# Summing two spectral products on VectorE ahead of the second half's inverse step, with a new hand-fixed order

## The chip, the cores and the metric

The kernel runs on one core of one Trainium2 chip. The metric is the time of one launch on the device in microseconds (us), lower is better. A core has five engines with queues of their own, which run at the same time and wait for each other through semaphores: PE (matrix multiply, TensorE), DVE (VectorE), ACT (ScalarE), POOL (GpSimd) and SP, which here only issues transfers (DMA). Matmul results land in PSUM, eight banks of 128 x 512 fp32, and DVE or ACT must copy or consume them before a bank can be used again.

## What is computed

Two blocks follow each other on a sequence of S = 2048 rows and D = 512 columns, in bf16. The first is a gated long convolution by FFT, the second a normalised mixer with an MLP. Cut to what matters:

```python
x = A_q;  qn = layernorm(x)
k_shift = sum over 4 taps of shifted k * shift_k
kv = k_shift * v
y = irfft(rfft(pad(kv)) * rfft(pad(ssm_k)))[:S] + kv * ssm_D      # length 2S
h = x + qn * y
u = layernorm(h);  h1 = gelu(layernorm(u) @ w1)                   # four column groups, shifted by -1, +1, -2, +2 rows
x1 = u + concat(shifted groups) @ w2
out = h + x1 + gelu(layernorm(x1) @ w3) @ w4                      # F = 1792
```

## The kernel before, in words

The rows are split into two halves, s = 0 and s = 1, of eight blocks of 128 rows each. Four signals are transformed: the filter's two halves (F0, F1) and kv's two halves (A0, A1). Each goes through the same stages, all matmuls with small trigonometric tables as weights, and a task in the code is one such step for one slice:

- S1 (`forward1`, `step1`, L389): the first transform step, evicted from PSUM by a copy E1 (`copy`, L257); X (L405): eight transfers from SBUF to SBUF that regroup the rows; S2 (`forward2`, L413): the second step, evicted by E2 (for F1 the eviction adds F0 in the same instruction, L425).
- P (`conv`, L474): the spectral products on DVE, 128 x 2048 bf16 each. The result of the first half needs one product of signals (A0 F0), that of the second two (A0 F1 and A1 F0). For each of four slices kl and each of two arrangements x of real and imaginary parts a product is one instruction: 8 for the first half, 16 for the second.
- I2 (L484): the inverse's first step on PE, 16 matmuls of 32 x 64 weights for each product, all products of a slice accumulating in the same four PSUM banks. EV copies the four banks out (L257, two copies), XI (L495) regroups by two transfers, I1 (L502) is the last inverse step, two blocks a time.

K and KV (L442, L450) make kv: matmuls with diagonal matrices of the taps (`dg`, L307 on DVE or L299 on POOL) and a product with v. Q (`qstat`, L506) takes the statistics of a block of q, QV, QP, QN (`qvar`, `qpow`, `qnorm`) turn them into scale and shift, Y (L613) normalises it. H (L616) joins q and y into h, one instruction on DVE for each block; HS (L600 or L602) takes its statistics; uw, rr, hn turn them into scale and shift (DVE and POOL); hb (L653, L655) writes the normalised block. LT and TE transpose it, some pairs of blocks with PE (L670 and a copy), five pairs of the two normalisations with transfers (`turn`: two writes to DRAM, L663, and a transposing read, L665). W and U (L699, L703) are w1 and its gelu, X2 and S (L722, L725) are w2 and its sum, SS, ux, r1, xn, lb, LX, EX repeat statistics, normalisation and transposes, M and G (L777, L781) are w3 and gelu, O and Z (L790, L792) are w4 and the last sum, OUT writes a block. R (L729) adds the residual.

All of these are about 780 tasks of a planner class, `Plan`. Nothing decides an order on the chip: the string ORDER lists the tasks, each with its engine letter and the numbers of the buffers it takes (PSUM banks, product buffers and others). `Plan.emit` goes through that list, so each engine runs its tasks in the order of the list, and a task that isn't ready holds up everything behind it on its engine. The numbers such as `{V: 1.15}` are the planner's costs in us, used outside this file when the list was made. A `port` note tells the planner of operations that use VectorE's and GpSimd's access to SBUF.

Around the change the order is as follows. The first half's convolution ends in I1 for s = 0, then H, W and X2 of the first half run while the second half's spectra are formed. From I2 of the second half on PE works off slice by slice, with M, G and O tasks of the first half's MLP between as other work. After its last I2 come two O tasks, then I1 for s = 1, then M tasks, two LT tasks and two O tasks, then W and X2 of the second half. After W of the second half almost only MLP matmuls remain.

Of the kernel before, what the change touches and what calls it, by code (L numbers as in the profile page):

```python
# [9 lines left out]
P = 128  # L10
S = 2048
D = 512
# [3 lines left out]
NB = 8  # L16
XW = 258
KW = NB * 129 + 8
# [13 lines left out]
004S 029P0 000S 002S 003S 005S 008S 031V 037V 001S 030P 063P23 006S 055P45 009S 057P67 064V 007S 056A 038G 065P01 010S 058A 019S 059P45 033V 045G  # L32
061P23 060A 087P60 039G 036V 062A 095P71 046V 042V 066A 093P4 032G 043V 047A 074S 101P5 044A 034G 015S 094V 051P23 022S 088V 053P01 035G 023S 052A
040V 072S 089P4 024S 054A 049G 091P6 021S 090V 073S 041A 097P2 096V 050G 070S 092V 099P3 048A 069S 102V 068S 107P01 098V 109P67 017S 100V 108A 103P45
067S 110V 111P23 018S 104A 115P01 071S 113P67 112A 323V 105P45 324V 116A 211P20 106V 114A 117P01 212V 119S 118A 084P4567 326V 085A 081P2301 123S 329V
086V 120S 083A 215P4 020S 082A 330V 124S 078P0167 327V 125S 217P5 080A 216V 121S 079A 075P2367 012S 218V 011S 325V 076A 127P4501 016S 319V 328V 122S
077A 219P21 129V 126S 331G 128A 013S 220V 130P6701 139V01 132A 141V23 131A 133P4501 332G 134A 140P23670 147V45 142P 135A 333G 149V67 143A 337G0
148P45011 155V01 150P 343G1 144A 145S 221P2 340G2 157V23 152A 146S 334G3 014S 151A 136P6701 222V 137V 138A 156P23452 153S 158P 154S 163V45 225P0 159A
223P1 160A 165V67 161S 164P67230 162S 226V 166P 224V 175P45 167A 168V 213P0 176A 169S 183P67 214V 170S 185P23 184A 187P45 315S 186V 177P01 188A 189P67
178V 179P23 190A 181P45 180V 171P67 028S 182A 172P01 338V 192S 231P45 196S 335V 339A 349G0 173P23 316S 344V 336A 346G3 193S 341V 235P67 232A 355G1  # L40
195S 347V 174P10 236A 352G2 191S 350V 237P45 198S 358G 342A 356V 202P6723 197S 348A 353V 194S 345A 359G 204V 239P01 238A 371G 203V 241P23 240A 227P45
242A 229P01 372G 360V 228V 230A 199P6723 247S 361G0 373V 233P45 351A 364G1 200V 362P00 234A 374G2 365P1 384V 366A 377G3 208P6745 245S 363V 354A 375P11
243S 201V 385G 367P0 376A 244S 357A 378P1 386V 246S 369P2 379A 390V0 318S 209V 397G 387A1 382P3 248S 370A 250S 388P12 210V 368A 398G 391P6 249S 380P7
383A 389A 027S 392V 399G 251P2345 263V01 381A 393P0 253A 026S 400G3 265V23 395P1 025S 252A 317S 403V2 205P6745 396A 267V45 401P23 394A 404P3 502P1
402A 206V 405A 506P0 503V 408P2 507V 504A 406P3 269V67 508A 409A 264P67011 558V 407A 266P 207V 268P 559G 270P 560G 498P2 271A 272V 561G1 510P3 564G0
499V 274S 494P4 501V 273S 562P50 511V 565P6 514P7 563A 495V 566A 411V 254P0123 496A 567P50 515V 256A 275V01 569P4 568A 577P6 277V23 570A 257P2345 578A
412V 573P7 259A 255V 571P6 258A 279V45 579P4 572A 574A 281V67 575P5 580A 516A 276P01232 414V 500A 278P 513V 280P 576A 615G 512V 282P 581P6 505V 283A
# [46 lines left out]
def body(ctx, tc, fx, kt, q, v, sd, w1, w2, w3, w4, out):  # L94
# [200 lines left out]
    def dg(c):  # L295
        def f(e, sl):
            if e == GP:
                tap = r_k[:, c * KW + NB * 129:(c + 1) * KW].rearrange("p (j x) -> p j x", x=2)[:, :, 1:2]
                pool.affine_select(out=diag[:, c], in_=tap.to_broadcast([P, 4, P]), compare_op=OP.is_equal, fill=0.0, base=0,  # L299
                                   pattern=[[0, 4], [-1, P]], channel_multiplier=1)  # L300
                return
# [542 lines left out]
```

## Time and profile before

| what | value |
|---|---|
| median of 3 runs | 213.93 us (213.45 to 215.72) |
| the profiled execution's own time | 213.26 us |
| its span, first to last instruction | 211.6 us |
| what lies around the span | 1.66 us |
| PE busy | 195.7 us, 93% |
| DVE busy | 144.8 us, 68% |
| ACT busy | 125.5 us, 59% |
| POOL busy | 80.1 us, 38% |

The profile's page has six parts. Part 1 gives busy time, part 2 cuts the span into 40 slices of 5.29 us and gives the busy share of each engine in tenths, part 4 is the chain of work that ended last, part 5 groups instructions by line, engine and tile. Other views used below are the chain in order of time, the timeline of one engine (start, duration, operation, and in brackets how long the engine was idle before it and on whom it waited), and a table of stretches of the span. PE takes in work all through the span, so what counts is in which stretch another engine keeps it waiting.

### The profile page before, as it was taken

Reading aid. Unit: us, or ns where it says so; the run is one execution under the profiler, and the core shown is the slowest. Engines: PE = TensorE matmul, PEld = TensorE weight load, DVE = VectorE, ACT = ScalarE, POOL = GpSimd, SP = SyncE. Lnnn points to the kernel's source line nnn. Section 1 sums busy time; section 2 is a strip of 40 time slices with the busy share of each in tenths; the row PEclk is TensorE's granted clock in tenths of the full one; section 3 lists DMA queues with packets and bytes.
Section 4 is the critical chain, followed back from the end, with each engine's and each line's share of the span. In section 5 each row is a group of like instructions: output and inputs, shape, how many; then the busy total and the mean of one; then the engine's idle time right before and its main releaser. Section 6 shows DMA issues by size and latency. Waiting matters only on the chain.

```text
span 211.6 us, 5040 instructions
## 1 busy us (share of the span) xinstructions
PE 195.7 (93%) x1964; PEld 116.2 (55%) x1980; DVE 144.8 (68%) x302; ACT 125.5 (59%) x206; POOL 80.1 (38%) x177
## 2 busy tenths in 40 slices
PE   6899769898889999979999999989999999999992
PEld 5454323442248546636744884645848888645450
DVE  6998999999999999999868971559972000112031
ACT  3979989787999658943751883364623565301010
POOL 7850059804888140287044683212765000000000
PEclk9999999999999999999999999999999999999999
DMA  6999895976948995000693008533146440010011
GB/s 173 313 403 397 321 325 222 256 205 237 371 169 294 332 435 147 0 28 13 89 232 92 27 22 181 98 69 82 42 107 154 102 74 0 3 50 34 16 50 50
DMA packets 30809, 32.86 MB, mean 155 GB/s; under 512 B 20545, under 2 KB 22594, under 8 KB 30530
## 3 DMA queue, kind: packets, MB, share of 16 engines
q1 hardware_dynamic: 30786, 32.55, 50.8%
q8 instruction: 15, 0.25, 0.5%
q14 instruction: 8, 0.07, 0.1%
HBM read 13.14 MB, written 4.46 MB: 83 GB/s over the span
## 4 chain that ended last, share of the span: by engine, by line
PE 59%; DVE 13%; ACT 12%; DMA 6%; issue 3%; POOL 3%; SPq 3%; DVEq 0%; ACTq 0%; POOLq 0%
PE ps L777 21%; PE ps L790 18%; ACT r_a L257 5%; PE ps L722 5%; PE ps L699 5%; PE ps L484 3%; DVE r_v L616 3%; DMA r_dg<-dhb 2%; DMA r_a<-r_a 2%; PE ps L502 2%; PE ps L413 2%; DMA r_k<-in_kt_dram 2%; DVE r_f L425 2%; DVE r_dg L307 1%; DVE r_p L474 1%
## 5 line engine op out<-in xcount | busy, mean ns | idle before, releaser
L777 PEld LDWEIGHTS <-r_k 128*128 128x128 bf16 x448 | 43.5, 98 | 7.7 <-issue 1.2
L792 DVE TENSOR_TENSOR r_v<-ps,r_v 128x512 bf16<-128x512 f32 x16 | 10.7, 686 | 42.4 <-PE ps L790 42.4
L474 DVE TENSOR_TENSOR r_p<-r_a,r_f 128x2048 bf16<-128x2048 bf16 x24 | 28.7, 1240 | 1.0 <-PE ps L484 0.6
L777 PE MATMUL ps<-r_dg,r_k 128*128 128x256 bf16 x224 | 25.6, 273 | 0.1
L257 ACT CAST r_a<-ps 128x1024 bf16<-128x1024 f32 x23 | 22.2, 1026 | 3.0 <-PE ps L413 2.8
L781 ACT ACTIVATE r_f<-ps 128x512 bf16<-128x512 f32 x14 | 7.8, 599 | 20.6 <-PE ps L777 20.6
L613 POOL TENSOR_SCALAR z_t<-r_q,qrs,qnm 128x512 f32<-128x512 bf16 x11 | 13.0, 1188 | 12.6 <-DVE r_v L616 12.0
L442 PE MATMUL ps<-r_dg,r_k 128*128 128x256 bf16 (+3 forms) x108 | 15.2, 284 | 1.6 <-ACT r_f L257 0.8
L257 ACT CAST r_vs<-ps 128x1024 bf16<-128x1024 f32 x14 | 13.7, 1032 | 4.9 <-PE ps L484 4.9
L725 DVE SCALAR_TENSOR_TENSOR r_q<-r_v,hrr,ps 128x512 bf16<-128x512 bf16 x16 | 11.4, 742 | 5.9 <-PE ps L722 3.7
L781 ACT ACTIVATE r_a<-ps 128x512 bf16<-128x512 f32 x14 | 7.8, 606 | 12.2 <-PE ps L777 12.2
L257 ACT CAST r_f<-ps 128x1024 bf16<-128x1024 f32 x14 | 13.2, 1023 | 3.0 <-PE ps L389 2.8
L442 PEld LDWEIGHTS <-r_k 128*128 128x128 bf16 x112 | 9.5, 98 | 9.5 <-issue 4.8
L484 PE MATMUL ps<-r_p,ttab 32*64 32x512 bf16 x384 | 13.3, 379 | 1.0 <-DVE r_p L474 0.8
L699 PEld LDWEIGHTS <-r_fx 128*128 128x128 bf16 x128 | 12.3, 98 | 3.2 <-DMA r_dg<-dhb 0.6
L600 ACT ACTIVATE junk<-r_v 128x512 bf16<-128x512 bf16 x14 | 8.9, 635 | 7.3 <-DVE r_v L616 7.1
L777 PE MATMUL ps<-xtx,r_k 128*128 128x256 bf16 x112 | 13.0, 273 | 0.0
L600 ACT ACTIVATE junk<-r_q 128x512 bf16<-128x512 bf16 x12 | 7.6, 630 | 9.2 <-DVE r_q L725 9.1
L777 PE MATMUL ps<-xty,r_k 128*128 128x256 bf16 x112 | 12.7, 272 | 0.0
L790 PE MATMUL ps<-w4s,r_f 128*128 128x512 bf16 x54 | 12.5, 379 | 0.1
L748 POOL TENSOR_TENSOR xrr<-xrr,mhalf 128x2 f32<-128x2 f32 x8 | 7.2, 900 | 14.2 <-DVE xrr L745 13.8
L389 PEld LDWEIGHTS <-f 128*32 128x32 bf16 x256 | 6.1, 95 | 11.3 <-issue 7.5
(183 smaller groups left out, 374.7 us busy)
## 6 DMA issues: line engine op xcount, KB each, us to landing
r_z<-r_vs SPq DMA_DIRECT2D x16, 256.0 KB, 3.9
r_k<-in_kt_dram SPq DMA_DIRECT2D x8, 260.0 KB, 4.6
r_v<-in_v_dram SPq DMA_DIRECT2D x4, 512.0 KB, 7.3
r_f<-r_f SPq DMA_DIRECT2D x8, 256.0 KB, 5.2
r_q<-in_q_dram SPq DMA_DIRECT2D x8, 256.0 KB, 5.7
r_a<-r_a SPq DMA_DIRECT2D x8, 256.0 KB, 4.2
r_f<-r_a SPq DMA_DIRECT2D x8, 256.0 KB, 4.2
r_a<-r_z SPq DMA_DIRECT2D x8, 256.0 KB, 4.1
```

The costliest lines, as they stand in the source:

```text
L257: (act.copy if e in "AM" else on[e].tensor_copy)(o, i)
L442: nc.tensor.matmul(o[:, (d + j0) * P:(d + j1 + 1) * P], lhsT=kT[s][c][:, bb, x:x + P], rhs=diag[:, c, j0:j1 + 1, :].rearrange("p j x -> p ...
L474: on[e].tensor_tensor(out=prs[:, sl[0]:sl[0] + 2, :, :], in0=sp[a][:, kl, :, :, :], in1=gv, op=MUL)
L484: nc.tensor.matmul(ps[64 * t:64 * t + 64, bk[h], :], lhsT=ttab[32 * h:32 * h + 32, 2 * kl + t, 2 if x else xx, :], rhs=prs[32 * h:32 * h + ...
L600: act.activation(junk[:], x, ACT.Square, accum_out=sq[:, i, 1:2])
L613: on[e].tensor_scalar(out=z_t[:, sl[0], :], in0=qs, scalar1=qrs[:, i:i + 1], scalar2=qnm[:, i:i + 1], op0=MUL, op1=ADD)
L699: nc.tensor.matmul(ps[:, sl[0], j * 256:(j + 1) * 256], lhsT=w1s[:, k, m * P:(m + 1) * P], rhs=xt[:, k, :], start=(k == 0), stop=(k == DC ...
L725: vec.scalar_tensor_tensor(out=q_sb[:, s, b, :], in0=h_sb[s][:, b, :], scalar=hrr[:, 4 * s + b // 2, 0, b % 2:b % 2 + 1], in1=ps[:, got((" ...
L777: nc.tensor.matmul(ps[:, sl[0], j * 256:(j + 1) * 256], lhsT=w3s[:, k, fc * P:(fc + 1) * P], rhs=xt[:, k, :], start=(k == 0), stop=(k == D ...
L781: act.activation(gb[:, 2 * fp:2 * fp + 2, :], ps[:, got(("M", s, p, fp))[0], :].rearrange("p (j x) -> p j x", j=2), ACT.Gelu_apprx_tanh)
L790: nc.tensor.matmul(ps[:, sl[0], :], lhsT=gb[:, fc, (b % 2) * P:(b % 2 + 1) * P], rhs=w4s[:, fc, :], start=(fc == 0), stop=(fc == FC - 1))
L792: add(("Z", s, b), {V: 0.61}, lambda e, sl, b=b: vec.tensor_tensor(out=h_sb[s][:, b, :], in0=ps[:, got(("O", s, b))[0], :], in1=h_sb[s][:, ...
```

## The change

Five things differ.

1. For the second half the two products of a slice and arrangement are added on DVE by a new task PA (128 x 2048 bf16, in place), and I2 runs on the sum. I2 of the second half has two tasks a slice in place of four: 8 tasks (128 matmuls) fewer on PE, 8 instructions more on DVE. The chain that forced the products into one fixed order (`last_p`) is gone, and the table `tt` is now awaited by the products.
2. The tap diagonals `dg` are all made by POOL; before, two of the four were made by DVE, four instructions each.
3. The statistics of four of the second half's q blocks are taken by ACT in two passes with accumulation, in place of one instruction on DVE each.
4. `qvar` for the second half has three more small instructions for these four blocks.
5. ORDER is a new list: engines, order and buffers of all tasks were chosen again, those of the transfers too.

```diff
-            if e == GP:
-                ...
-            for j in range(4):
-                ...
-        add(("dg", c), {V: 0.8, A: 1.19, GP: 0.85}, dg(c), [("Lk", 0, c)], port="VG")
+        add(("dg", c), {GP: 0.65}, dg(c), [("Lk", 0, c)], port="VG")
...
-                    add(("P", s, kl, i, x), {V: 1.15}, f, [("E2", y, kl, t) for y in (a, g) for t in range(2)] + ["f2"] + before, take=[("pr", -1)], port="VG")
-                    last_p.append(("P", s, kl, i, x))
-                    first, last = (i, x) == (0, 0), (i, x) == (len(prods) - 1, 1)
+                    add(("P", s, kl, i, x), {V: 1.15}, f, [("E2", y, kl, t) for y in (a, g) for t in range(2)] + ["f2", "tt"], take=[("pr", -1)], port="VG")
+                    first, last, y = x == 0, x == 1, ("P", s, kl, 0, x)
+                    if i < len(prods) - 1:
+                        continue
+                    if i:
+                        def f(e, sl, x=x, kl=kl):
+                            pa, pb = (prs[:, got(("P", s, kl, j, x))[0]:got(("P", s, kl, j, x))[0] + 2, :, :] for j in range(2))
+                            vec.tensor_tensor(out=pa, in0=pa, in1=pb, op=ADD)
+                        add(("PA", s, kl, x), {V: 1.135}, f, [y, ("P", s, kl, i, x)], drop=[(("P", s, kl, i, x), 0)], port="VG")
+                        y = ("PA", s, kl, x)
...
-                    add(("I2", s, kl, 2 * i + x), {PEc: 0.44}, f,
-                        ["tt"] + [...] if first else [("I2", s, kl, 2 * i + x - 1)],
+                    add(("I2", s, kl, x), {PEc: 0.44}, f, [y] if first else [y, ("I2", s, kl, 0)],
...
 def qstat(s, b):
-    return lambda e, sl: vec.bn_stats(qst[:, 8 * s + b, :], q_sb[:, s, b, :])
+    if s == 0 or b < 4:
+        return lambda e, sl: vec.bn_stats(qst[:, 8 * s + b, :], q_sb[:, s, b, :])
+    def f(e, sl):
+        act.activation(junk[:], q_sb[:, s, b, :], ACT.Identity, accum_out=qst[:, 8 * s + b, 0:1])
+        act.activation(junk[:], q_sb[:, s, b, :], ACT.Square, accum_out=qst[:, 8 * s + b, 1:2])
+    return f
...
-            add(("Q", s, b), {V: 0.6}, qstat(s, b), [("Lq", s, b // 2)])
+            add(("Q", s, b), {A: 1.3} if s and b > 3 else {V: 0.6}, qstat(s, b), [("Lq", s, b // 2)])
```

The places in the new list that the prediction speaks of, in the notation of the tasks (half or signal, slice, part):

- DVE from the first H of the first half to the last PA: 8 PA more than before; 5 Q, 5 R, 2 E2 copies and 1 Z fewer; the small tasks (hn, hb, lb, uw, xn, two transposes' copies) go both ways. Between the last PA and the first H of the second half stand 4 R and 1 Q more, 1 Y and 1 Z fewer.
- ACT in the same stretch: all of the second half's four new Q, two more E2 copies, two more transposes' copies. One Q stands between the last gelus G and the two EV of the last slice. The last EV pair of the first half (slice 3) is on ACT; before, ACT and DVE shared it.
- PE: S1.A1.3.1, the last matmuls of the A1 signal's first step, stand behind the first W task. After the last I2 again two O tasks, then I1 for s = 1. The first W task whose transposed input comes by transfer (W.1.1) stands behind LT.1.0, LT.1.1, the last I1, two O and W.1.0; before, that task (W.1.2) stood behind LT.1.0, LT.1.1, one M, W.1.0, two O and two X2.
- SP: the load of w1 (Lw1) stands behind the eight X of F1, before it stood ahead of them; Lw2 stands ahead of all X of A1; w4 (Lw4) is issued ahead of the last X of A1, with Lw3. At the start the second load of v (Lv.0.1) moves from 11th to 15th place.

More of the change, by code (lines that the diff above doesn't have):

```diff
@@ L36 @@
[L36 to L43, printed above, removed]
@@ L461, in kvsrc @@
         return lambda b: kvs[:, got(("K", 2 * s + b // 4, 0), "kv")[0], b % 4, :]
-    last_p = []
     def conv(s, prods):
@@ L469, in conv @@
                 for x in range(2):
-                    before = last_p[-1:]
                     def f(e, sl, a=a, g=g, x=x, kl=kl):
```

81 lines of the change are left out of this document (44 added, 37 removed).

## Prediction

> **What bounds the kernel now.** I read the page first: busy shares and the 40 slices.
>
> ```profile
> span 211.6 us, 5040 instructions
> PE 195.7 (93%) x1964; PEld 116.2 (55%) x1980; DVE 144.8 (68%) x302; ACT 125.5 (59%) x206; POOL 80.1 (38%) x177
> ...
> PE   6899769898889999979999999989999999999992
> ...
> DVE  6998999999999999999868971559972000112031
> ACT  3979989787999658943751883364623565301010
> ```
>
> PE is at 9 in most slices from the tenth on, so it looks as if PE alone counted. But DVE stands at 9 from the third slice to the 19th (until about 100 us): up to there two engines are full at once, and only behind it is PE alone. Then I asked for stretches with borders at events: the first I1 (48.5), the second half's first I2 (73.7), its last I2 (107.7), the end of W for the second half (139.2). The first columns are the stretch, its length and PE's busy time; the third from the end is the granted clock. The events are read from the chain in order of time, below.
>
> ```profile
> core 0: us, PE busy (x) PEld busy (x) DVE busy (x) ACT busy (x) POOL busy (x), PEclk, DMA share, GB/s
> 48.50:73.70 25.20, 23.37 (x262) 12.20 (x264) 24.35 (x57) 21.82 (x42) 16.61 (x32) 1.00 0.78 278
> 73.70:107.70 34.00, 32.75 (x474) 19.96 (x478) 32.83 (x50) 22.15 (x37) 12.26 (x22) 1.00 0.44 130
> 107.70:139.20 31.50, 30.89 (x213) 19.77 (x209) 20.64 (x71) 17.16 (x36) 15.55 (x25) 1.00 0.45 93
> 139.20:207.80 68.60, 67.84 (x449) 43.92 (x452) 21.62 (x48) 24.04 (x48) 11.72 (x22) 1.00 0.26 62
> ```
>
> From 73.7 to 107.7 PE lacks 1.25 us of 34 and DVE 1.17: neither can give much without the other. Behind 139.2 PE has 0.76 us free in 68.6, and the change leaves that stage the same matmuls. So the end moves by what the end of W moves, and I follow four events to it.
>
> ```profile
> 49.66 1.87 DVE r_v L616 x5
> ...
> 105.86 1.87 PE ps L484 x64
> ...
> 107.89 5.99 PE ps L790 x27
> ...
> 113.92 3.61 PE ps L502 x16
> 117.53 5.24 PE ps L777 x48
> 122.77 0.24 PE ps L670 x4
> ...
> 130.83 4.84 DMA r_dg<-dhb
> ```
>
> **What goes from PE.** One slice's I2 is 64 matmuls in 1.87 us; half of it for four slices is 4 x 0.93 = 3.7 us off PE's sum. That is the most that the edit itself can give.
>
> **What comes to DVE.** The columns behind the bar are busy us and mean ns.
>
> ```profile
> L474 DVE TENSOR_TENSOR r_p<-r_a,r_f 128x2048 bf16<-128x2048 bf16 x24 | 28.7, 1240 | 1.0 <-PE ps L484 0.6
> ...
> L506 DVE BATCH_NORM_STATS2 qst<-r_q 128x6 f32<-128x512 bf16 x16 | 10.4, 682 | 0.9 <-DMA r_q<-in_q_dram 0.9
> ...
> L729 DVE SCALAR_TENSOR_TENSOR r_v<-r_q,hnm,r_v 128x512 bf16<-128x512 bf16 x16 | 11.5, 740 | 0.1
> ...
> L257 DVE CAST r_a<-ps 128x1024 bf16<-128x1024 f32 x9 | 10.8, 1214 | 0.4 <-PE ps L389 0.3
> ...
> L307 DVE TENSOR_SCALAR r_dg<-ident,r_k 128x128 bf16<-128x128 bf16 x8 | 3.1, 466 | 0.5 <-DMA r_k<-in_kt_dram 0.5
> ```
>
> A PA has the shape of a product: 8 x 1.24 = 9.9 us more. From the first H of the first half to the last PA the new list takes out 5 Q (3.4), 5 R (3.7) and 2 E2 copies (2.4), 9.5 together; the small tasks, each under 0.7 us, go both ways and I take them as 0, give or take 1. So DVE needs about as long as before for this stretch, 49.66 to 105.67 (next rows), for all that was moved. The R are only moved behind it.
>
> *Start of the first H.* DVE loses the diagonals (3.1) and gets one copy (1.2) and one KV more ahead of the first half's last product: up to 1.2 us earlier. Against it: POOL makes two more diagonals ahead of its tables, Lv.0.1 lies four places later, and ACT copies the last EV pair alone (1.93 us by its row below, where one copy of 1.2 on DVE ran beside). I take 0, between -1.2 and +1.0 (a late load as the 0.9 at L506).
>
> **The last I2 and I1.**
>
> ```profile
> 101.04 4.63 DVE L474 TENSOR_TENSOR r_p<-r_a,r_f 128x2048 bf16<-128x2048 bf16 x4 [0.63 <-PE ps L484]
> ...
> 105.58 1.87 DVE L506 BATCH_NORM_STATS2 qst<-r_q 128x6 f32<-128x512 bf16 x3
> ...
> 110.11 0.17 DVE L535 TENSOR_TENSOR qsd<-qsd,qrs 128x8 f32<-128x8 f32 x1 [1.75 <-POOL qrs L529]
> ...
> 113.97 0.69 DVE L792 TENSOR_TENSOR r_v<-ps,r_v 128x512 bf16<-128x512 f32 x1 [0.73 <-PE ps L790]
> 114.62 0.75 DVE L616 SCALAR_TENSOR_TENSOR r_v<-ps,qsd,z_t 128x512 bf16<-128x512 f32 x1
> ...
> 107.78 1.93 ACT L257 CAST r_vs<-ps 128x1024 bf16<-128x1024 f32 x2 [1.03 <-PE ps L484]
> ...
> 50.46 0.63 ACT L600 ACTIVATE junk<-r_v 128x512 bf16<-128x512 bf16 x1 [1.39 <-DVE r_v L616]
> ...
> 51.21 0.63 ACT L600 ACTIVATE junk<-r_v 128x512 bf16<-128x512 bf16 x1
> ```
>
> Before, the last product ended at 105.67 and the last I2 at 107.73, 2.06 later, because PE came to that slice only at 105.86. After, the last sum ends at about 105.7 and one I2 (0.47) follows: 106.2, or 106 to 107.6 if PE is the later one. So of PE's 3.7 us some 1.5 arrive, and the rest becomes waiting of PE for sums, or of other stages. Behind that I2 PE has its two O tasks (5.99), to 112.2. I1 also needs EV and XI: a pass with accumulation takes 0.63 and the next began 0.75 behind its start (50.46, 51.21), so a moved Q, two passes, costs ACT 1.5 us. Four are 6.0 against 34 - 22.15 = 11.9 us that ACT had free in that stage: covered, except that one stands close before the last EV. EV then ends 0 to 1 us later behind I2 than before (1.93 + 0 to 1); XI needs 3.9 from issue to landing (below). 106.2 + 1.9 + 0.5 + 0.1 + 3.9 = 112.6: I1 starts at 112.6, where it was 113.92. If this cover is gone, each late us of EV is one of I1.
>
> *The H of the second half.* Between the last product and the first H there were 114.62 - 105.67 = 8.95 us on DVE, 1.75 + 0.73 of them idle. New there: 4 R and a Q (3.0 + 0.7), gone a Y and a Z (about 1.2): 6.5 + 2.5 = 9.0, the idle time now filled. H starts at 105.7 + 9.0 = 114.7, less 0.6 if the small tasks fall well: nothing gained, or 0.6. The moved R are late here.
>
> *W of the second half.*
>
> ```profile
> 133.44 1.91 PE L699 MATMUL ps<-r_dg,r_fx 128*128 128x256 bf16 x16
> ...
> 135.71 1.92 PE L699 MATMUL ps<-r_dg,r_fx 128*128 128x256 bf16 x16 [0.36 <-DMA r_dg<-dhb]
> 137.47 1.91 PE L699 MATMUL ps<-xtx,r_fx 128*128 128x256 bf16 x16
> ```
>
> From H there lead statistics, POOL's power, hb, a write and a transposing read to the W whose input comes by transfer. Before, the first of these began at 133.44, 19.5 us behind I1's start, and the second was held 0.36 us by a transfer of 4.84. In the new list PE is at the first after three I1 (2.7), seven M (6 of them took 5.24, so 6.1), two LT (0.5), the last I1 (0.9), two O (6.0) and W.1.0 (two tasks, 1.7): 17.9 us, so 1.6 sooner behind I1, while the chain starts no sooner. From 112.6 that is 130.5, and the input was good for 133.4 before, so PE should wait there for 1 to 3 us, which takes up its lead. I put W's end 0.8 earlier, 138.4 in place of 139.2. X2 behind it loses a wait of 0.42 (next row), and the transfer EX.0.6, with two X2 moved behind W.1.1, may cost about that much.
>
> ```profile
> 140.02 6.98 PE L722 MATMUL ps<-r_fx,r_f 128*128 128x512 bf16 x30 [0.42 <-ACT r_f L703]
> ...
> DMA to landing us min/median/max: 3.1/3.9/4.8
> ...
> 60.01 1.03 ACT L257 CAST r_z<-ps 128x1024 bf16<-128x1024 f32 x1
> ...
> 66.55 0.62 PE L413 MATMUL ps<-r_a,ftab 64*32 64x512 bf16 x16
> ...
> DMA to landing us min/median/max: 2.6/4.3/9.1
> ```
>
> (The first landing row is XI's in this stage, the last that of all X.)
>
> **Sum.** First H 0, last I2 -1.5, of which H and W let 0.8 through: 213.26 - 0.8 = 212.5 for the profiled execution. That execution lay 0.67 under the median of 213.93; between the two bases I say **212.7 us**.
>
> **A rule against the change.** The busy POOL operation slows beside DVE's products:
>
> ```profile
> 34.31 7.06 POOL L613 TENSOR_SCALAR z_t<-r_q,qrs,qnm 128x512 f32<-128x512 bf16 x4
> ...
> 50.52 3.03 POOL L613 TENSOR_SCALAR z_t<-r_q,qrs,qnm 128x512 f32<-128x512 bf16 x4 [9.15 <-DVE r_v L616]
> ```
>
> Four take 7.06 us beside products and 3.03 beside H: 1.0 each. Eight PA can so hold up eight POOL operations by 1.0, 8 us, in a stage where POOL is busy 12.26 of 34; on the path there are hardly any, so I add nothing. The Trainium skill (SBUF — State Buffer, Who interferes with whom) says that a VectorE operation with two SBUF inputs blocks a GpSimd one that reads SBUF for its whole length; the rows agree, and by it the sum stays as it is.
>
> **Rivals.**
>
> *All of it arrives.* The small tasks fall well (-1), the first H comes 1.2 earlier, and the transposing chain is no later than PE: PE stays the only bound. 213.26 - 3.7 = 209.6. For it speaks that PE is full wherever the chain passes; against it, that DVE's sum doesn't shrink.
>
> *A late transfer ahead of S2.A1 (slower).* The last copy of A1 now stands behind a W task that needs w1, and w1 is loaded behind eight transfers of F1. Before, that copy ran from 60.01 to 61.0, and S2.A1.0 began at 66.55. Now ACT has two statistics (1.5), a gelu and two transposes' copies (0.5 each, of which about half displace what stood there before) between: I put its end at 63.6, and X.A1.1.0 lands 4.3 later, at 67.9. PE has about 0.9 us less ahead of S2.A1.0 and would be there at 65.7. I count the wait of 2.2 us as slack, since DVE's sums hold PE later anyway. With the longest landing, 9.1, it is 72.7, 4.8 more, of which about 0.6 are slack: 212.7 + 4.2 = 216.9. It decides from a landing of 8.3 us on (3.4 us over the forecast). PE would then also stand idle for over 5 us, and the granted clock, 1.00 in every stretch so far, could fall. The Trainium skill (TensorE: Matmul & The Clock Gate, What's actually happening) halves the clock after an idle window of about 3.4 us; no run here shows that, and it would be an estimate of 1.7 us more.
>
> *Nothing reaches the end.* ACT, with 6 us more, is late with EV by 2 to 3, and I1 begins where it did: 213.3 to 213.9. For it: ACT is at 8 or 9 before 55 us; against it: 11.9 us free.
>
> **How the numbers follow.** My forecast 0.36, nothing reaches the end 0.14, all arrives 0.28, late transfer 0.22. One per cent, about what a measurement of this kernel tells from no change, is 2.1 us. So faster 0.28, same 0.50, slower 0.22. The likeliest case alone spans 211.6 to 213.7. The range takes in both outer cases: 209.5 to 216.9.
>
> **What would show it.** Right: DVE without gaps from 50 to 105 and its last sum near 105.7; I2 at L484 with 256 matmuls; PE waiting on DVE's sums at I2 and on a transposing transfer at the first W of the second half; I1 near 112.6. Wrong: the last sum before 104 (then the first rival), PE idle over 4 us ahead of an L413 group near 66 (the second), or EV ending over 3 us behind the last I2 (the third).

## The result, and the profile after

The changed kernel takes 216.72 us (median of 12 runs, 215.48 to 218.55), the kernel before 214.38 us beside it (12 runs, 213.35 to 216.14). The ratio is 1.0101, 95% interval 1.0063 to 1.0139: the change costs 2.3 us, 1.0%. Measured a second time (after_again below) the ratio is 1.0092 (1.0062 to 1.0121). Some runs of a kernel come over 1.5% above its fastest; the ratios leave them out, the medians below are of all runs, and the profiles of late_sp and start2, which are of such runs, are not read. All ratios are to the kernel before on the same chip, where its own median lay between 213.94 and 214.38, so runs of different chips are compared by their ratios.

The head of the page after, and its slices:

```profile
span 215.6 us, 4842 instructions
...
PE 194.2 (90%) x1852; PEld 115.7 (54%) x1852; DVE 147.8 (69%) x297; ACT 135.8 (63%) x226; POOL 77.9 (36%) x190
...
PE   6898868698876998999999999789999999999992
...
DVE  6678978987999999999999988448919000021221
ACT  3487979989999778998991891442643456421000
```

PE has 1.5 us less busy time than before and the span is 4.0 us longer, so 5.5 us more of it is PE without work. Most of the gaps are in the first 16 of PE's 40 slices. To place them I cut both profiles at four events: the first product, the end of the last product or sum, the second half's first I1, and the start of M.0.3, the first M behind W and X2 of the second half. The table of stretches, first the kernel before (columns: stretch, its length, busy time of the engines, granted clock, share of the transfer engines, GB/s):

```profile
core 0: us, PE busy (x) PEld busy (x) DVE busy (x) ACT busy (x) POOL busy (x), PEclk, DMA share, GB/s
0.00:30.43 30.43, 25.39 (x317) 13.92 (x328) 27.22 (x62) 24.92 (x29) 13.26 (x69) 1.00 0.91 320
30.43:105.67 75.24, 69.58 (x938) 37.56 (x928) 72.66 (x118) 58.34 (x93) 39.54 (x62) 1.00 0.63 203
105.67:113.92 8.25, 8.05 (x94) 3.70 (x94) 5.71 (x17) 3.00 (x5) 3.73 (x3) 1.00 0.86 191
113.92:146.83 32.91, 31.97 (x210) 20.06 (x213) 22.44 (x71) 19.75 (x44) 12.02 (x23) 1.00 0.37 81
146.83:211.50 64.67, 60.74 (x417) 40.98 (x419) 16.79 (x37) 19.52 (x37) 11.53 (x21) 1.00 0.23 56
```

And the changed kernel, cut at the same events:

```profile
0.00:33.78 33.78, 26.76 (x323) 14.03 (x324) 26.08 (x54) 23.99 (x28) 17.77 (x76) 1.00 0.88 300
33.78:109.27 75.49, 66.86 (x842) 36.98 (x840) 71.10 (x109) 68.42 (x114) 32.50 (x58) 1.00 0.61 203
109.27:116.74 7.47, 7.36 (x62) 3.30 (x62) 7.16 (x20) 3.73 (x8) 1.64 (x1) 1.00 0.53 128
116.74:150.91 34.17, 32.26 (x213) 20.37 (x213) 25.89 (x81) 17.86 (x36) 15.58 (x34) 1.00 0.36 71
150.91:215.60 64.69, 60.95 (x421) 41.02 (x419) 17.59 (x36) 21.84 (x43) 10.44 (x23) 0.99 0.23 61
```

Read by rows: the first product comes 3.35 us later. From it to the last sum takes 0.25 more than it took to the last product, with DVE busy 94 to 97% of it in both. I1 follows 0.78 sooner. The stage from I1 through W and X2 takes 1.26 more. The rest is the same. The sum is +4.1 for this pair of profiles. In the second row PE's busy time has fallen from 69.6 to 66.9 and the row is as long as before: that is where the edit's saving went, into PE's waiting. The waits are ahead of the saving, not behind it: PE is idle 3.31 us from the first product to the first I1 (2.58 before), 3.99 from the first H to the second half's first I2 (1.77 before), and 1.33 from there to the last sum (1.25 to the last product before).

Cut at the first I1 in place of the first product (52.33 us, before 48.50), 3.8 of the pair's 4.1 us lie ahead of the cut. The first H, which the prediction starts from, comes behind that I1, at 49.66 before and here at 53.03:

```profile
53.03 0.75 DVE L622 SCALAR_TENSOR_TENSOR r_v<-ps,qsd,z_t 128x512 bf16<-128x512 f32 x1 [1.52 <-PE ps L496]
```

The sums and I2 themselves are as expected; the view of the two lines gives count, minimum, median and maximum in ns:

```profile
L470 DVE TENSOR_TENSOR r_p<-r_p x8: 1207/1225/1226, 76.5 to 108.0; 128x2048 bf16<-128x2048 bf16 x8
```

```profile
L479 PE MATMUL ps<-r_p,ttab x256: 371/374/399, 35.9 to 110.1; 32*64 32x512 bf16 x128
```

The timeline of PE behind the last sum (start, duration, operation):

```profile
109.25 1.23 PE L479 MATMUL ps<-r_p,ttab 32*64 32x512 bf16 x32
110.41 6.22 PE L796 MATMUL ps<-w4s,r_v 128*128 128x512 bf16 x28
116.74 2.53 PE L496 MATMUL ps<-r_z,f 128*128 128x512 bf16 x11
```

Both I2 tasks of the last slice run there, since PE was still at M until 109.25. I1 follows the two O at once, so EV and XI were in time. And PE at W and X2 of the second half, with the idle time before each group in brackets:

```profile
134.75 1.91 PE L705 MATMUL ps<-r_dg,r_fx 128*128 128x256 bf16 x16
136.52 1.89 PE L728 MATMUL ps<-r_fx,r_h 128*128 128x512 bf16 x8
139.56 1.91 PE L705 MATMUL ps<-r_dg,r_fx 128*128 128x256 bf16 x16 [1.16 <-DMA r_dg<-dhb]
...
144.87 5.34 PE L728 MATMUL ps<-r_fx,r_f 128*128 128x512 bf16 x24 [0.75 <-ACT r_f L709]
```

Two waits, 1.16 for the second transposing transfer and 0.75 for a gelu, stand where the kernel before had 0.36 and 0.42.

### The profile page after: what moved, and what is told of

Same layout as the page of the kernel before. It is cut to its first block, busy times and chain, and to the rows that moved or that the text cites. A ratio compares the mean times of both kernels' runs of the same rounds, so it can differ in the third digit from the quotient of the medians.

```text
span 215.6 us, 4842 instructions
## 1 busy us (share of the span) xinstructions
PE 194.2 (90%) x1852; PEld 115.7 (54%) x1852; DVE 147.8 (69%) x297; ACT 135.8 (63%) x226; POOL 77.9 (36%) x190
## 4 chain that ended last, share of the span: by engine, by line
PE 59%; ACT 10%; DMA 5%; DVE 4%; issue 2%; ACTq 0%
PE ps L783 21%; PE ps L796 21%; PE ps L705 5%; PE ps L728 4%; PE ps L496 3%; ACT r_z L257 2%; DMA r_dg<-dhb 2%; PE ps L479 2%; DVE r_p L462 2%; DMA r_z<-r_vs 2%; ACT r_vs L257 2%; DVE r_q L731 2%; ACT junk L606 2%; DMA r_a<-r_z 1%; PE ps L405 1%
## 5 line engine op out<-in xcount | busy, mean ns | idle before, releaser
L257 ACT CAST r_a<-ps 128x1024 bf16<-128x1024 f32 x27 | 26.2, 1020 | 2.3 <-PE ps L405 1.3
L619 POOL TENSOR_SCALAR z_t<-r_q,qrs,qnm 128x512 f32<-128x512 bf16 x9 | 9.2, 1028 | 19.6 <-DVE r_v L622 17.4
L257 ACT CAST r_f<-ps 128x1024 bf16<-128x1024 f32 x12 | 11.5, 1028 | 7.3 <-PE ps L381 6.5
L606 ACT ACTIVATE junk<-r_q 128x512 bf16<-128x512 bf16 x13 | 8.3, 636 | 9.6 <-DVE r_q L731 9.5
L381 PEld LDWEIGHTS <-f 128*32 128x32 bf16 x256 | 6.7, 102 | 13.9 <-issue 9.5
L442 DVE TENSOR_TENSOR r_kv<-ps,r_v 128x512 bf16<-128x512 f32 x16 | 10.5, 685 | 3.6 <-DMA r_v<-in_v_dram 2.0
L796 PE MATMUL ps<-w4s,r_v 128*128 128x512 bf16 x56 | 12.6, 379 | 0.0
L796 PE MATMUL ps<-w4s,r_a 128*128 128x512 bf16 x56 | 12.6, 379 | 0.0
L796 PE MATMUL ps<-w4s,r_kv 128*128 128x512 bf16 x56 | 12.4, 379 | 0.0
```

The source lines that it names most:

```text
L257: (act.copy if e in "AM" else on[e].tensor_copy)(o, i)
L442: vec.tensor_tensor(out=kvs[:, got(("K", g, 0), "kv")[0], :, c * P:(c + 1) * P], in0=ps[:, got(("K", g, c))[0], :].rearrange("p (b x) -> p ...
L606: act.activation(junk[:], x, ACT.Square, accum_out=sq[:, i, 1:2])
L619: on[e].tensor_scalar(out=z_t[:, sl[0], :], in0=qs, scalar1=qrs[:, i:i + 1], scalar2=qnm[:, i:i + 1], op0=MUL, op1=ADD)
L796: nc.tensor.matmul(ps[:, sl[0], :], lhsT=gb[:, fc, (b % 2) * P:(b % 2 + 1) * P], rhs=w4s[:, fc, :], start=(fc == 0), stop=(fc == FC - 1))
```

## The experiments

The same four events, read from the timelines of the profiles, for all runs used below. All times in us.

| run | first product | to last product or sum | to I1, second half | to M.0.3 | to the end | median | ratio (95%) |
|---|---|---|---|---|---|---|---|
| before | 30.43 | 75.24 | 8.25 | 32.91 | 64.7 | 214.38 | 1 |
| changed | 33.78 | 75.49 | 7.47 | 34.17 | 64.7 | 216.72 | 1.0101 (1.0063-1.0139) |
| after_again | 33.02 | 75.24 | 7.48 | 34.12 | 64.7 | 216.31 | 1.0092 (1.0062-1.0121) |
| sums_in_old | 31.27 | 85.97 | 6.68 | 34.28 | 64.7 | 224.79 | 1.0500 (1.0463-1.0536) |
| no_sums | 33.25 | 76.79 | 10.32 | 33.93 | 64.7 | 219.96 | 1.0275 (1.0236-1.0315) |
| old_start | 30.97 | 75.97 | 7.49 | 34.41 | 65.1 | 215.97 | 1.0086 (1.0059-1.0113) |
| loads_first | 35.91 | 75.34 | 7.53 | 34.11 | 64.7 | 219.90 | 1.0296 (1.0248-1.0344) |
| two_loads | 34.99 | 75.04 | 7.50 | 34.56 | 64.7 | 218.32 | 1.0182 (1.0140-1.0223) |
| late_sp | | | | | | 215.36 | 1.0037 (1.0004-1.0071) |
| late_dve | 33.93 | 75.84 | 7.48 | 34.20 | 65.1 | 217.17 | 1.0106 (1.0045-1.0167) |
| late_all | 31.16 | 75.09 | 7.50 | 33.72 | 64.7 | 215.61 | 1.0045 (1.0018-1.0073) |
| late_sp_only | 33.02 | 75.70 | 7.49 | 33.83 | 64.7 | 215.66 | 1.0058 (1.0029-1.0087) |
| k_early | 32.05 | 75.17 | 7.46 | 34.29 | 64.7 | 215.53 | 1.0043 (1.0012-1.0075) |
| k_early_late_sp | 32.61 | 75.16 | 7.46 | 33.76 | 64.7 | 214.79 | 0.9977 (0.9938-1.0017) |
| start2 | | | | | | 215.46 | 1.0055 (1.0022-1.0088) |
| best2 | 32.23 | 75.61 | 7.47 | 32.40 | 64.7 | 213.59 | 0.9965 (0.9937-0.9992) |

### The sums alone, and all but the sums

The diffs are in the names of the tasks, by engine. sums_in_old is the kernel before with the new `conv` and nothing else:

```diff
-DVE: P.1.kl.0.x ... P.1.kl.1.x
+DVE: P.1.kl.0.x ... P.1.kl.1.x PA.1.kl.x
-PE:  I2.1.kl.0 I2.1.kl.1 I2.1.kl.2 I2.1.kl.3
+PE:  I2.1.kl.0 I2.1.kl.1
```

> The kernel before, in its own order, with the sums alone: each of the eight PA right behind its second product on VectorE, eight I2 tasks less on TensorE, no statistics or residuals moved away. Theory 1, VectorE sets the stretch from the first H to the last sum: eight sums of 1.23 us are 9.9 us more there, the last sum ends near 115.5, less the 0.9 us that I2 ends sooner behind it; the time is 220 to 224 us. Theory 2, TensorE sets that stretch, with 92% of it busy: the sums fill waits and 3.7 us of matmuls go; the time is 211 to 215 us.

It takes 224.79 us, ratio 1.0500: theory 1. The stretch from the first product to the last sum, and a piece of it:

```profile
31.27:117.24 85.97, 70.32 (x858) 37.66 (x849) 82.87 (x126) 59.65 (x94) 41.67 (x62) 0.96 0.60 189
```

```profile
95.00:110.00 15.00, 12.88 (x122) 6.59 (x110) 14.41 (x19) 5.76 (x7) 10.93 (x14) 0.89 0.10 26
```

The stretch is 10.7 us longer than before, DVE's busy time in it 10.2: eight sums of 1.23 lie on the path in full. PE, with less to do, waits, and in the second row its granted clock is down to 0.89 (what brought it down is not shown). So the edit by itself is bad by 10 us; what makes it bearable is the work that the new list takes away from DVE.

no_sums is the opposite: the changed kernel with four I2 a slice again and no sums, I2 put beside their products.

```diff
-DVE: P.1.kl.0.x ... P.1.kl.1.x PA.1.kl.x
+DVE: P.1.kl.0.x ... P.1.kl.1.x
-PE:  I2.1.kl.0 I2.1.kl.1
+PE:  I2.1.kl.0 I2.1.kl.1 I2.1.kl.2 I2.1.kl.3
```

> The changed kernel without the sums: the second half's four products of a slice each go through their own I2 as in the kernel before (eight I2 tasks more, 3.7 us on TensorE), with the I2 tasks put beside their products on TensorE; what was moved away from VectorE stays away. Theory 1, VectorE sets that stretch: without 9.9 us of sums the last product ends 4 to 8 us sooner than 109.27 and the time is 211 to 215 us, below the changed kernel. Theory 2, TensorE sets it: the last product ends within 2 us of 109.3, and the 3.7 us come back; the time is 217 to 220 us.

219.96 us, ratio 1.0275, 3.2 to 3.6 above the changed kernel's two medians (3.7 to 3.9 by the ratios): theory 2. The stretch:

```profile
33.25:110.04 76.79, 68.12 (x907) 36.08 (x912) 62.03 (x101) 66.63 (x109) 27.42 (x59) 1.00 0.59 198
```

DVE has 9 us less to do than in the changed kernel and the stretch is 1.3 us longer; then I1 comes 2.8 us later behind the last product, because M tasks stand ahead of the last slice's I2 on a PE that is never idle there. (Where I2 stands among the M was my choice; another place could make this run somewhat faster.) Both results together: this stretch has two full engines, and in these orders to take work off one of them alone gives nothing. The sums trade 3.7 us of PE for 9.9 of DVE, the moved statistics, residuals and copies pay the 9.9 back, and what is left is 0.

### The start

The first product is late in the changed kernel. old_start puts the whole stage up to the first I1 back, in the order of the kernel before, two diagonals on DVE included:

```diff
-all engines, tasks ahead of the first I1: order of the changed kernel
+all engines, tasks ahead of the first I1: order of the kernel before
-        add(("dg", c), {GP: 0.65}, dg(c), [("Lk", 0, c)], port="VG")
+        add(("dg", c), {V: 0.8, A: 1.19, GP: 0.85}, dg(c), [("Lk", 0, c)], port="VG")
```

> The changed kernel, with the stage up to the first I1 in the order of the kernel before (and two of the four diagonal tables back on VectorE, as there). The sums, the moved statistics and everything after the first I1 stay as changed. Theory 1, the loss is made at the start and carried: the first H comes at 49.7 us (as before) in place of 53.03, everything after it 3.3 us earlier, the time is 216.7 - 3.3 = 213.4 us (212.4 to 214.4), about the kernel before. Theory 2, the late part loses it by itself (the transposing transfers ahead of W, the statistics on ScalarE): the first H is at 49.7 all the same, but W.1.3 stays near 141.3 and the time is 215.7 to 217.

215.97 us, ratio 1.0086: the time is theory 2's, but not the trace, where W.1.3 starts at 139.24 and does not stay near 141.3. The first product is at 30.97, close to the kernel before, but the next stretch is 0.5 us longer than in the changed kernel and the last 0.3. The median lies only 0.3 to 0.8 below the changed kernel's two, and by the ratios it is 0.1 to 0.3: the old start alone gives back hardly anything. The first two profiles had misled me. The old start is not always as early as 30.43: the five profiles read that have it show 30.43, 31.27, 30.97, 33.93 and 31.16, 31.55 on average, and the four with the new start 33.78, 33.02, 33.25 and 33.02, 33.27 on average. By these averages the start costs 1.7 us, not 3.35. But the 33.93 is late_dve's, whose granted clock was low shortly before:

```profile
25.00:30.00 5.00, 4.34 (x52) 1.76 (x34) 3.74 (x6) 3.62 (x4) 0.00 (x0) 0.66 0.90 300
```

In the other eight it was 1.00 from 0 to 30 us. Without late_dve the old start's average is 30.96, and the new start costs 2.3 us. after_again, the changed kernel without any edit, asked whether the late start was chance:

> The changed kernel once more, beside the next three on the same chip. In four profiles of one and the same start (old-start and the three runs built on it) the first I1 came at 49.41, 50.93, 51.34 and 48.59, so a single profile places the start only to about 1.4 us. If the loss of the change sits in its start, the first I1 is again above 51.3 (52.33 and 51.98 in the two profiles so far) and the time from there to the end is 163 to 164 us, as in the kernel before (163.1); if the late 52.33 was chance, the first I1 is at 48.5 to 51.

Its first I1 came at 52.01 and the time from there to the end was 162.6 (163.1 in the kernel before): the late start is no chance, and in this profile nothing is lost behind the first I1.

Which part of the start is it? Here PE at the start, before and then changed; the last row of each is the first K:

```profile
4.82 1.48 PE L389 MATMUL ps<-r_fx,f 128*32 128x512 bf16 x24 [0.33 <-DMA r_fx<-in_fx_dram]
...
7.80 1.41 PE L442 MATMUL ps<-r_dg,r_k 128*128 128x512 bf16 x8 [0.21 <-DVE r_dg L307]
```

```profile
6.38 4.01 PE L381 MATMUL ps<-r_fx,f 128*32 128x512 bf16 x40 [1.06 <-DMA r_fx<-in_fx_dram]
10.32 1.86 PE L434 MATMUL ps<-r_dg,r_k 128*128 128x512 bf16 x13
```

The second group of S1 waits for its load, which now stands behind two loads of k, and K begins 2.5 us later. loads_first moved the loads of F ahead:

```diff
-SP: Lk.0.2 Lf.0.2 Lk.0.3 Lf.0.1 Lf.0.3 Lk.0.0 Lk.0.1 Lv.0.0 Lk.1.0 ... Lf.0.0 Lsd Lv.0.1
+SP: Lf.0.2 Lf.0.1 Lf.0.3 Lsd Lk.0.0 Lk.0.2 Lk.0.1 Lk.0.3 Lf.0.0 Lv.0.0 Lv.0.1 Lk.1.0 ...
-SP: X.F0.0.3 X.A0.0.2 ... Lf.1.3 Lv.1.0
+SP: X.F0.0.3 Lv.1.0 X.A0.0.2 ... Lf.1.3
```

> The changed kernel with nothing but the queue of loads at the start in another order: the three Lf that the first matmuls read and Lsd go ahead of the Lk, both halves of the first Lv ahead of the second half's Lk and of Lq, and Lv.1.0 ahead of the X.A0 transfers. Theory 1a, the order of the loads on a full transfer system makes the late start: the first cast on ScalarE comes near 5.5 us in place of 7.47, the first product at 31 to 32 in place of 33.78, the time falls by 2 us to 214.7. Theory 1b, it is the order of the compute engines at the start, or the second half's loads that then stand behind: the first product stays within 1 us of 33.78 and the time within 1 us of 216.7.

219.90 us, worse by 3.2 than the changed kernel (4.2 by the ratios). The first cast was early (4.91 in place of 7.47), and then:

```profile
10.81 1.74 PE L434 MATMUL ps<-r_dg,r_k 128*128 128x512 bf16 x7 [3.43 <-POOL r_dg L298]
```

PE waits 3.43 us for the diagonals. POOL makes dg.3 first, and the load that it reads, Lk.0.3, was now the last of the four. two_loads left the first eight loads and brought Lf.0.0 and Lv.0.1 forward, with the tasks that hang on them (the diff shows the main places):

```diff
-SP: ... Lk.0.1 Lv.0.0 Lk.1.0 Lk.1.3 Lq.0.2 Lq.0.1 Lf.0.0 Lsd Lv.0.1 X.F0.1.0 ...
+SP: ... Lk.0.1 Lv.0.0 Lf.0.0 Lsd Lv.0.1 Lk.1.0 Lk.1.3 Lq.0.2 Lq.0.1 X.F0.1.0 ...
-PE: K.0.1 K.1.1 K.1.3 K.0.3 S1.F0.0.0 S1.F0.0.1
+PE: K.0.1 S1.F0.0.0 S1.F0.0.1 K.1.1 K.1.3 K.0.3
```

> The changed kernel with two loads brought forward: Lf.0.0 (with Lsd) and Lv.0.1 go right behind Lv.0.0, ahead of the second half's Lk and of Lq; what hangs on Lf.0.0 follows it (dr ahead of f2v on GpSimd, the matmuls S1.F0.0 behind K.0.1, both their casts on ScalarE behind tts, the X.F0.0 transfers ahead of Lq.0.3), and Q.0.3 moves behind KV.1.0. Theory 1, the start is late because these two land at 14.06 and 16.62 (8.24 and 13.19 before), which holds VectorE at KV.1.3 for 1.34 us and bunches the X.F0.0 transfers with X.A0: they land by 11 and 13, the first product comes at 31 to 32 in place of 33.78, the first I1 at 49.5 to 50.5, the time falls by 1.5 to 2.5 us. Theory 2, the chain through the diagonal tables on GpSimd and K sets the start: the first product stays within 0.7 us of 33.78, the time within 0.7 us of the changed kernel.

218.32 us, worse by 1.6 to 2.0; theory 1 is refuted. Both loads did land early (11.15 and 12.45). DVE shows what took their place:

```profile
18.24 0.69 DVE L442 TENSOR_TENSOR r_kv<-ps,r_v 128x512 bf16<-128x512 f32 x1 [2.13 <-PE ps L434]
```

The KV that had waited 1.34 us for Lv.0.1 now waits 2.13 for a K, since the S1 that I had moved up stands ahead of it on PE. In both failures it is K that got later. So k_early puts everything in the order in which the chain Lf, S1, diagonal, K, KV needs it:

```diff
-SP:   Lk.0.2 Lf.0.2 Lk.0.3 Lf.0.1 Lf.0.3 Lk.0.0 Lk.0.1 Lv.0.0 Lk.1.0 ... Lf.0.0 Lsd Lv.0.1
+SP:   Lf.0.2 Lf.0.1 Lf.0.3 Lk.0.0 Lk.0.2 Lk.0.1 Lv.0.0 Lk.0.3 Lv.0.1 Lf.0.0 Lsd Lk.1.0 ...
-POOL: ftv dg.3 dg.0 dg.2 dg.1 f2v dr
+POOL: dg.0 dg.2 dg.1 ftv dg.3 f2v dr
-DVE:  ttv tta fta KV.0.0 Q.0.3 f2a KV.0.2 KV.0.1 KV.1.3 KV.0.3 KV.1.0
+DVE:  ttv tta KV.0.0 KV.0.2 KV.0.1 fta f2a KV.1.3 KV.0.3 KV.1.0 Q.0.3
-ACT:  ft tts
+ACT:  tts ft
```

> The changed kernel with the start rearranged for the chain Lf, S1.F0, diagonal tables, K, KV: loads in the order Lf.0.2, Lf.0.1, Lf.0.3, Lk.0.0, Lk.0.2, Lk.0.1, Lv.0.0, Lk.0.3, Lv.0.1, Lf.0.0, Lsd; on GpSimd three tables ahead of ftv in the order in which their Lk land; on VectorE the first three KV ahead of fta. Theory 1, TensorE's chain through S1.F0 into K sets the start (K began at 10.32 in the changed kernel, 7.80 before, and at 10.81 where the loads of F came first but the tables last): K begins at 7.5 to 8.5, the first product at 31 to 32, the first I1 at 49.5 to 50.5, the time 1.5 to 2.5 us below the changed kernel. Theory 2, the transfers of X.F0 and X.A0 behind it set it: K begins earlier and the first I1 stays above 51.5, the time within 0.7 us.

```profile
7.73 6.26 PE L434 MATMUL ps<-r_dg,r_k 128*128 128x512 bf16 x48
```

K begins at 7.73 without a wait, the first product comes at 32.05, 1.2 earlier than the average of the changed start, and the time is 215.53, 0.8 below after_again beside it (ratio 1.0043 against 1.0092, the intervals overlap). Its first I1 is at 50.61, between the theories. Theory 1 by its mechanism; by its size half of what I expected, since K gained 2.6 us and the product 1.2. start2 went on along the same chain:

```diff
-DVE: KV.1.0 Q.0.3 Q.0.4 E1.F0.0.1 KV.1.1 KV.1.2
+DVE: KV.1.0 KV.1.1 KV.1.2 E1.F0.0.1 Q.0.3 Q.0.4
-PE:  K.0.3 S1.F0.0.0 S1.F0.0.1 S1.A0.1.0 S1.A0.1.1 K.1.2
+PE:  K.0.3 K.1.2 S1.F0.0.0 S1.F0.0.1 S1.A0.1.0 S1.A0.1.1
```

> The kernel with the rearranged start (K early), and three more places in it: KV.1.1 and KV.1.2 go ahead of Q.0.3 on VectorE, which waited 1.62 us for its load there, E1.F0.0.1 right behind them, and K.1.2 goes up to the other K on TensorE. Theory 1, the chain K, KV, S1.A0, X.A0 sets the start all the way: with KV.1.2 done near 17 in place of 20.54 the X.A0 transfers are issued 1 to 2 us sooner, the first product comes at 30.3 to 31.3 in place of 32.05, the first I1 at 49 to 50, as in the kernel before, the time 0.8 to 1.6 us below that kernel's 215.53. Theory 2, the transfer system, busy with loads until 28 us, sets what is left: the first I1 stays above 50.3, the time within 0.4 us.

215.46 us, within 0.1 of k_early, and by the ratio no better (1.0055 for 1.0043): theory 2. best2 has the same start, and its profile is read here. The transfers X.A0 in k_early and then in best2 (duration of the issues, first and last start; landing behind the issue; the rows include two transfers of X.F0 and one):

```profile
L397 SPq DMA_DIRECT2D r_a<-r_a x8: 530/635/1330, 22.5 to 31.0; - x8
...
DMA to landing us min/median/max: 4.3/5.0/6.1
```

```profile
L397 SPq DMA_DIRECT2D r_a<-r_a x8: 524/582/805, 21.3 to 30.6; - x8
...
DMA to landing us min/median/max: 6.3/6.9/7.5
```

X.A0.1.0 was issued 1.7 us sooner (22.83 for 24.56) and landed 0.2 us later (30.01 for 29.83). The next two rows are the transfer system of best2 from 12 to 20 and from 20 to 30 us:

```profile
12.00:20.00 8.00, 7.13 (x91) 3.80 (x89) 8.00 (x13) 6.60 (x9) 3.46 (x6) 1.00 1.01 374
20.00:30.00 10.00, 7.11 (x101) 3.02 (x100) 8.06 (x12) 9.09 (x11) 2.33 (x9) 1.00 0.94 340
```

It is full, and a transfer issued sooner stands longer in the queue. The Trainium skill (DMA: Bandwidth & Descriptors, Queues, rings and completion order) says that each transfer engine takes the descriptors of a queue in the order of the ring; the trace agrees: the loads and the X all go through SP's one queue here, and of those issued up to 31 us in these two profiles every landing that the traces have comes in the order of issue. The earlier issue bought no earlier landing. Whether fewer loads ahead of X.A0 would bring the product below 31.5 was not tried.

### The late stage

late_sp and late_sp_only change one place in SP's queue, on old_start and on the changed kernel:

```diff
-SP: LT.1.4 OUT.0.0 TE.1.2 LT.1.5 LT.1.7 LT.1.6 TE.1.4 TE.1.6
+SP: LT.1.4 LT.1.5 TE.1.2 LT.1.7 LT.1.6 TE.1.4 TE.1.6 OUT.0.0
```

> The kernel with the old start, and one change in SyncE's queue late in the second half: LT.1.5 goes ahead of TE.1.2 and OUT.0.0 behind the three TE. In the old-start run LT.1.5 stood behind TE.1.2 until 130.48 though its source was ready at 127.85, and W.1.2 waited 1.40 us for TE.1.4. Theory 1, the queue is what makes W late: TE.1.4 issues by 131.6 in place of 132.63, the wait of 1.40 falls to 0.5 or less, everything after it comes 0.9 to 1.4 us earlier. Theory 2, the writing of the transposed halves takes its time whatever their order (the second landed 3.7 us after its issue there): the wait stays over 1 us, the time within 0.5 us of the old-start run.

> The changed kernel with nothing but LT.1.5 put ahead of TE.1.2 in SyncE's queue and OUT.0.0 behind the TE. Theory 1, the queue makes W.1.2 late: its wait (1.16 us in the changed kernel) goes, from the second half's first I1 to the start of M.0.3 are 33.0 us in place of 34.2 (32.9 in the kernel before), and the time falls by 1.1 us. Theory 2, it does not carry: those stay at 34, the time within 0.4 us.

Both medians are 0.6 us below the kernel that they change (215.36 for 215.97, 215.66 for 216.31); by the ratios late_sp is 1.0 us below, as theory 1 has it, and late_sp_only 0.7, between the theories, and the intervals overlap. In late_sp_only's profile TE.1.4 was issued 0.9 us sooner behind I1 (17.33 for 18.22 in after_again) and landed 0.3 sooner (22.45 for 22.73); PE's wait fell from 1.11 to 0.83. So the queue counts for a little, and most of it is the transfer itself: the second transposing transfer takes 4.5 to 5.1 us from issue to landing (4.5 in after_again, 5.1 here), the first 2.8 to 3.3, in every profile read but best2's, where the second took 3.2. late_sp_only, late_all and k_early_late_sp have best2's queue there and show 5.1, 4.9 and 5.0, so the queue does not make it short. What sets this is open.

late_dve and late_all change DVE behind the last sum; late_all has late_sp's queue and the order of X2 as well:

```diff
-DVE: PA.1.3.1 Q.1.2 R.0.2 Q.1.3 Q.1.0 R.0.3 Q.1.1 QV.1 Z.0.2 R.0.0 Z.0.0 R.0.4 R.0.5 QN.1
+DVE: PA.1.3.1 Q.1.2 Q.1.3 Q.1.0 Q.1.1 QV.1 R.0.2 R.0.3 Z.0.2 R.0.0 Z.0.0 QN.1
-PE:  X2.1.3 X2.1.0 X2.1.6 X2.1.2
+PE:  X2.1.3 X2.1.2 X2.1.0 X2.1.6
```

> The kernel with the old start, and one change on VectorE behind the last sum: the four Q and QV.1 go ahead of the R and Z, and R.0.4 and R.0.5 behind the second half's H. In the old-start run the first H of the second half came at 116.29 with VectorE busy without a gap since the last sum, though I1 had ended at 115.45. Theory 1, VectorE is what H waits for there: the first H comes at 115.2 to 115.5, the chain through hb to the transposing transfers 0.8 to 1.1 us earlier, the wait of W.1.2 (1.40) shrinks by as much, and so does the time. Theory 2, the transfers behind it set W: H is earlier and W.1.2 is not; the time within 0.4 us of the old-start run.

> The kernel with the old start and both late edits (LT.1.5 ahead in the queue, Q and QV ahead of R on VectorE), and X2.1.2 with its S ahead of X2.1.0, which waited 0.75 us for the gelu of W.1.3. If the two late waits add up, W.1.2 and X2.1.0 no longer wait and the time is 1.8 to 2.2 us below the old-start run, at the kernel before (213.5 to 214.5). If something else stands behind them (the second transposing transfer, ScalarE's gelus), less than 1 us goes, 215 to 216.

late_dve: the first H is 0.8 us closer behind I1 (1.06 for 1.86), W.1.2 waits 1.39 as before (1.40), and the stage is 0.2 shorter: theory 2 by the trace (its time, 217.17 from four runs, is too uncertain to tell). H of the second half is late in the changed kernel and costs 0.2 us at most. late_all: X2.1.0 no longer waits, W.1.2 still does (1.53), and the stage is 0.7 shorter, as long as the gelu's wait was. 215.61 us, the second case.

### Both repairs

k_early_late_sp joins k_early's start and late_sp's queue; best2 joins start2's start, late_sp's queue and the order of X2.

> Both edits of the last two together: the start rearranged and LT.1.5 ahead. If the changed kernel loses 2.5 us at the start and 1.2 us at the transposing transfers and nothing else, this one is 2.6 to 3.6 us below it and 0.3 to 1.5 us below the kernel before: 213 to 214 us. If the start doesn't yield, it is 1.1 us below the changed kernel, near 215.5.

> The same start, LT.1.5 ahead in SyncE's queue, and X2.1.2 with its S ahead of X2.1.0, which waited 0.75 us for a gelu. If the start yields once more and the two waits of W and X2 go, the time is 212.5 to 214, 0.2 to 0.9% below the kernel before: what the sums with their moved statistics are worth when the order around them loses nothing (I1 of the second half came 0.8 us sooner behind the last sum than behind the last product). If the change is worth nothing in itself, it ends within 0.3% of the kernel before.

k_early_late_sp: 214.79 us, ratio 0.9977 (0.9938 to 1.0017), as fast as the kernel before; its median lies between the two cases expected, its ratio in the first. best2: 213.59 us, ratio 0.9965 (0.9937 to 0.9992), in the range expected though its start, with the first product at 32.23, had not yielded once more. It is the only version that is faster than both kernels, by 0.35%, and the interval ends close to 1. Two of its stretches:

```profile
32.23:107.84 75.61, 67.00 (x842) 36.90 (x840) 71.40 (x109) 68.55 (x114) 32.44 (x58) 1.00 0.60 203
...
115.31:147.71 32.40, 32.29 (x212) 20.30 (x213) 25.99 (x81) 17.75 (x36) 14.46 (x31) 1.00 0.40 78
```

In the second PE is busy 32.29 of 32.40: both waits are gone, and the stage is 1.8 us shorter than in the changed kernel. The wait at X2 went with the order of X2 (late_all has none there either). The wait at W went because the second transposing transfer landed in 3.2 us in this profile; k_early_late_sp, with the same queue, still waits 0.73 there, so it is not shown that the edit removes it. The first stretch is as long as ever.

## Why the prediction was wrong

The forecast was 212.7 us and no measurable change; the kernel is slower by 1.0%. That 216.72 us still lies inside the stated 209.5 to 216.9 is luck: the upper end came from a late transfer ahead of S2.A1, and that is not what happened. Step by step:

- *What goes from PE, what comes to DVE.* Right. 256 matmuls are left, a sum takes 1.23 us, and from the first product to the last sum DVE needs as long as before (75.49 and 75.24 in the two profiles).
- *Start of the first H: "I take 0, between -1.2 and +1.0".* This is the step that failed. The first H came at 53.03 in place of 49.66. In all four profiles of the new start it lies between 52.68 and 53.03, in those of the old start between 49.32 and 50.54 (52.07 in late_dve's). Of this the first product is 1.7 us late on average, or 2.3 without late_dve's profile; the rest comes between it and the first I1, where DVE is idle 2.2 to 2.9 us with the new start and 0.4 to 1.0 with the old. I had seen that Lv.0.1 lies later and that POOL makes two more diagonals, and priced them by the longest wait for a load that the old trace had, 0.9. I had not followed the other loads: Lf.0.1 goes behind two loads of k, K begins 2.5 us later. From the first product to the last sum DVE is busy 94% of the time and makes up none of it. How much of the kernel's 2.3 us the start carries by itself is open, for with the old start back only 0.1 to 0.3 us came back by the ratios (old_start). Taking 0 for a stage whose whole list was new was no estimate.
- *The last I2 and I1.* Right behind the last sum: I1 7.47 us after it (predicted 6.9, before 8.25), EV in time. PE came later than the sum, 1.2 us as in the second of the two values I gave. PE never waits for a sum; I had expected such waits at I2. Its missing work shows as waits elsewhere, ahead of the second half's first I2.
- *The H of the second half.* 1.86 us behind I1, as predicted (2.1). late_dve shows that it costs 0.2 us at most.
- *W of the second half.* The lead was right: PE is at the first transferred W 18.0 us behind I1 (17.9 predicted), but doesn't wait there. It waits at the second, 1.16, and 0.75 at X2 for a gelu, where I had expected a wait to go. Predicted from I1 to W's end were 25.8 us, measured are 26.5, and the whole stage to M.0.3 is 1.26 longer than before. So what I1 gains is lost again here, in the old order as in the new: from the last product or sum to M.0.3 are 41.16 us before, 41.64 and 41.60 in the two profiles of the changed kernel, and 40.96 in sums_in_old, where I1 comes 1.6 us sooner and W and X2 wait 1.12 and 0.97. I had let I1, W and X2 together give 0.8; they lost 0.5.
- *Sum.* Start +1.7 (+2.3 without late_dve's profile), products to last sum +0.2 (75.48 on the average of three profiles, 75.24 before), I1 -0.8, W and X2 +1.2: +2.3 us (+2.9), against 2.3 and 2.0 measured. The sum is no proof, for all terms but the start rest on one profile of the kernel before, an execution of 213.26 us where the median is 214.38.
- *Rivals.* "All of it arrives" fails, as DVE's stretch doesn't shrink. "A late transfer ahead of S2.A1" is not what happened either, though its 216.9 is near the measured time: PE waits 1.17 there, under the 2.2 that I had called slack, and the stretch is no longer for it.

```profile
70.13 0.63 PE L405 MATMUL ps<-r_a,ftab 64*32 64x512 bf16 x16 [1.17 <-DMA r_a<-r_z]
```

"Nothing reaches the end" was in substance the nearest: PE's 3.7 us reach nothing. Its mechanism, a late EV, is not what happened: EV was in time.

What is shown: that DVE sets the middle (sums_in_old) and PE sets it too (no_sums), that 3.8 of the pair's 4.1 us, and in after_again's profile the whole loss, lie ahead of the first I1, that the chain into K makes about half of the first product's lateness (1.2 of 1.7 to 2.3, k_early), and that without the two waits the stage of W and X2 is 1.8 us shorter (best2's profile). Not shown is that the start alone carries the loss. Open are the other half of the first product's lateness, why old_start gained so little, and why the second transposing transfer takes 3.2 us in one profile and 4.5 to 5.1 in the others.

## What to carry to other kernels

Where two engines are both full in a stretch, as here, expect nothing from work that goes from one to the other, however cheap the trade looks on the first. When an edit comes with a new order of everything, price each stage of that order from its own loads and queues, the start too, for a full engine behind it makes up little of a loss. And place events of a start that hangs on loads by several profiles, not by one, with their granted clock beside them.

## What the runs showed of the hardware

- One and the same start puts the first product at 30.4 to 31.3 us in four profiles and at 33.9 in a fifth (late_dve), whose granted clock was 0.66 from 25 to 30 us; the changed start, though later, stays within 33.0 to 33.8 (four).
- With the transfer system at a share of 0.91 to 1.01 from 12 to 30 us, an X issued 1.7 us sooner landed no sooner (k_early and best2).
- Of two transposing transfers of the same size, issued 2.5 to 3.9 us apart, the first takes 2.8 to 3.3 and the second 4.5 to 5.1 us to land, in all profiles read but best2's (3.2).
- In sums_in_old, where PE was busy 12.88 of 15 us, its granted clock fell to 0.89 in that stretch; in the stretches of the changed kernel and of the one before it was 0.99 or more. In k_early it was 0.66 from 40 to 45 us, with PE busy 4.61 of 5. What sets it off is not shown.
